# A Fourier mixing layer with an expert MLP: first load, spectrum layout and last tiles changed

## The chip, the cores and the metric

The kernel runs on one core of one Trainium2 chip. The time is the device time of one execution in microseconds. A profile of one execution gives the span from the first to the last instruction and what each engine did. The engines are TensorE (PE), VectorE (DVE), ScalarE (ACT), GpSimd (POOL) and SyncE (SP). SP, ACT and POOL can issue DMAs.

## The reference, cut to what matters

x has 8 batches of 2496 positions with 256 channels.

```python
X = np.fft.rfft(x, axis=1)
Yr = Xr @ w_r - Xi @ w_i + b_r          # complex 256 x 256 product per frequency
Yi = Xr @ w_i + Xi @ w_r + b_i
Y* = sign(Y*) * max(|Y*| - 0.01, 0)     # soft threshold of both parts
y = np.fft.irfft(Y, n=2496, axis=1)
e = argmax(mean(y, axis=1) @ w_gate)    # one expert of 8 for each batch
out = gate * (relu(y @ w1[e]) @ w2[e])  # 256 -> 1024 -> 256
```

## The kernel before

The transform of 2496 positions is split as 39 x 64. A batch goes through these steps; the names are those of the tiles, the lines those of the profile.

- x is loaded as `xin` (L265) from POOL's DMA queue, cast to fp16 on the way. Batch 0 is loaded in nine pieces, three groups of columns times three groups of 39 partitions; other batches in three.
- The DFT over 39 gives `pa`. In batches 0 and 1 ("direct", L424) it is evacuated into `XB` (L435). In batches 2 to 7 (L537) it goes to `A` (L547), is written to DRAM as `fwd` (L559, L564) and read back in another order as `XB` (L578), since the second transform needs other partitions.
- Direct batches multiply with the weights first (`pm` L460, evacuated as `Pt` L471) and then make the DFT over 64 (`pb` L488 and L490, with the tables `tf` and `tm`). The others make the DFT first (`px` L601, evacuated as `XT`), then three products (`pm` L639) that DVE joins with the bias (`tt` L653, `z` L662).
- DVE thresholds `z` into `Y` (L513 or L681).
- The inverse transform over 64 with the table `ti` gives `pv` (L382), evacuated as `V` (L390), two frequencies at a time. Each V is stored to the DRAM tile `scr` (L395). When all ten are stored, four DMAs read them back with the frequencies on 120 partitions (`V2`, L708 and L711; the profile cuts the number off and calls this tile V as well).
- The inverse over 39 with `wi` gives `pi` (L734), evacuated as `ysb` (L749, L755): y of the batch.
- The MLP goes over chunks of 512 positions, the last of 448. Eight pairs of matmuls per chunk give `ph` (L863), relu makes `hs` (L875 on ACT, L877 on DVE), and `po` (L896) multiplies with the second weights, scaled by the gate on evacuation into `ost` (L928 or L931) and stored from SP (L952).
- The last chunk leaves a tile of 64 rows. Its eight products (L907) go in two halves of four to PE columns 0 to 63 and 64 to 127, so that they can run beside each other; ACT evacuates the tile before (L928), DVE scales one half (L938) and adds the other (L941), and SP stores both (L957, L959).

The expert is found from the zero frequency as soon as that is there; POOL then reads its index and loads the weights `w1s` and `w2s` (L815, L820).

The order of all instructions is written out by a planner (`Schedule`). Each operation has an engine, a guessed duration, what it depends on, and a due time `vt`. The planner goes through simulated time, picks the engine (ACT or DVE) for evacuations, and emits the instructions in the order that it found. Times at which the first loads land are given to it as constants (`X0_AT`, `X1_AT`, `W_AT`, `T_AT`). What it emits on an engine runs in that order, each instruction waiting for its semaphores. PSUM has five banks for tag "a", two for "h" and one for "o". The load of x of batch b is held until `V2` of batch b-2 has been read: a POOL copy of one element of V2 into the new `xin` tile stands ahead of it.

Of the kernel before, what the change touches and what calls it, by code (L numbers as in the profile page):

```python
# [16 lines left out]
P = 128  # L17
B = 8
# [16 lines left out]
def _tables():  # L35
# [22 lines left out]
    wi = wi.reshape(120, 117)  # L58
# [9 lines left out]
    tf[:, :, 0, 1], tf[:, :, 1, 1] = -s * sg, c * sg  # L68
    def lay(m):
        return np.ascontiguousarray(  # L70
            m.reshape(NK1, P, P).transpose(1, 0, 2)).astype(np.float16)
# [11 lines left out]
    return wa.astype(np.float16), wi.astype(np.float16), lay(tf), lay(ti)  # L83
# [21 lines left out]
class Schedule:  # L105
# [17 lines left out]
    def op(self, eng, occ, emit, vt, deps=(), lat=None, allocs=(), dma=0.0):  # L123
        o = Op((eng,), {eng: occ}, {eng: occ if lat is None else lat}, emit, vt,
               list(deps), list(allocs), dma)
        self.ops.append(o)
        return o
# [32 lines left out]
    def run(self):  # L160
        free = dict.fromkeys(("PE", "ACT", "DVE", "SP", "POOL"), 7.0)
        ring = {"SP": 7.0, "POOL": 24.0}
# [44 lines left out]
def kernel(  # L207
# [14 lines left out]
    wa_np, wi_np, tf_np, ti_np = _tables()  # L222
    d_wa = nc.inline_tensor(wa_np, name="d_wa")
    d_wi = nc.inline_tensor(wi_np, name="d_wi")
    d_tf = nc.inline_tensor(tf_np, name="d_tf")
    d_ti = nc.inline_tensor(ti_np, name="d_ti")
# [9 lines left out]
    XROW = 2 * D + 16  # L236
    BUFS = {"XT": 2, "hs": 2, "z": 3, "V": 6}
# [19 lines left out]
    def load_now(b, cuts, hold=None):  # L257

        xin = xpool.tile([117, NG // 2, XROW], FP16, name="xin")
        if hold is not None:  # L260
            nc.gpsimd.tensor_copy(out=xin[0:1, 0, 0:2], in_=hold)
        xv = x[b].rearrange("(a n) c -> a n c", n=N2)
        for c0, c1 in zip(cuts, cuts[1:]):
            for j in range(3):
                nc.gpsimd.dma_start(  # L265
                    out=xin[39 * j : 39 * j + 39, c0:c1, 0 : 2 * D],
                    in_=xv[:, 21 * j + 2 * c0 : 21 * j + 2 * c1, :].rearrange(
                        "a (g i) c -> a g (i c)", i=2))
        return xin

    wa = cpool.tile([117, 120], FP16, name="wa")
    nc.sync.dma_start(out=wa, in_=d_wa.ap())
    xin0 = load_now(0, (0, 4, 8, NG // 2))
# [3 lines left out]
    nc.gpsimd.dma_start(out=wm, in_=w_i.rearrange("(t p) c -> p t c", p=P))  # L277
    tf = cpool.tile([P, NK1, P], FP16, name="tf")
# [6 lines left out]
    for k0, k9 in ((0, 4), (4, 12), (12, 20)):  # L285
        nc.gpsimd.dma_start(out=tf[:, k0:k9], in_=d_tf.ap()[:, k0:k9])
        nc.vector.tensor_scalar_mul(out=tm[:, k0:k9, 0:64],
                                    in0=tf[:, k0:k9, 64:P], scalar1=-1.0)
        nc.vector.tensor_copy(out=tm[:, k0:k9, 64:P], in_=tf[:, k0:k9, 0:64])
        if k0 == 0:  # L290
            for i, bv in enumerate((b_r, b_i)):
                nc.gpsimd.dma_start(
                    out=bias[:, i],
                    in_=bass.AP(tensor=bv.tensor, offset=bv.offset,
                                ap=[[0, P], [1, D]]))
        nc.gpsimd.dma_start(out=ti[:, k0:k9], in_=d_ti.ap()[:, k0:k9])
    bias2 = cpool.tile([P, D], FP32, name="bias2")
    nc.vector.tensor_copy(out=bias2[0:64], in_=bias[0:64, 0])
    nc.vector.tensor_copy(out=bias2[64:P], in_=bias[64:P, 1])
# [3 lines left out]
    nc.vector.tensor_copy(out=w4[:, :, 2], in_=wr)  # L303
    nc.scalar.copy(out=w4[:, :, 3], in_=wm)  # L304
    nc.vector.tensor_sub(out=w4[:, :, 0], in0=wm, in1=wr)
    nc.vector.scalar_tensor_tensor(out=w4[:, :, 1], in0=wr, scalar=-1.0, in1=wm,
                                   op0=ALU.mult, op1=ALU.subtract)
# [6 lines left out]
    xin1 = load_now(1, (0, NG // 2))  # L314
# [3 lines left out]
    nc.vector.tensor_copy(out=wg16, in_=wg)  # L318


    X0_AT, X1_AT = (9.5, 12.0, 14.0), 26.0
    W_AT, T_AT = 16.5, (18.0, 20.0, 21.0)
# [15 lines left out]
    w_in = [S.fixed(W_AT)]  # L338
# [6 lines left out]
    xdone = {0: [S.fixed(t) for t in X0_AT], 1: [S.fixed(X1_AT)]}  # L345
# [7 lines left out]
    def add_load(b):  # L353
        def emit(_):

            hold = V2_t[b - 2][0:1, 20, 0:2]
# [5 lines left out]
        o.after = xdone[b - 1][0] if b > 2 else None  # L362
# [9 lines left out]
    def add_inverse_b(b, k0, cell, oy, vt):  # L372
# [14 lines left out]
        def ev(eng):  # L387
            if b not in scr_t:
                scr_t[b] = dpool.tile([P, NK1, D], FP16, name="scr")
# [4 lines left out]
        def st(_):  # L394
            nc.sync.dma_start(out=scr_t[b][:, k0 : k0 + 2, :], in_=hc["V"])  # L395
# [5 lines left out]
    def add_attn_direct(b):  # L401
# [5 lines left out]
        for gb in range(6):  # L407
            gs = range(4 * gb, min(4 * gb + 4, NG))
            nq = 12 if gb < 5 else 4
            for ch in range(2):  # L410
# [3 lines left out]
                def mm(_, gs=gs, ch=ch, cell=cell):  # L414
# [6 lines left out]
                    for i, g in enumerate(gs):  # L421
# [7 lines left out]
                         vt(0.02 * gb), deps=[xd[min(gb // 2, len(xd) - 1)]],  # L429
# [14 lines left out]
        for kp in range(NK1 // 2):  # L444
# [61 lines left out]
            oz = S.op("DVE", 0.61, z_, v, deps=[m], lat=0.74)  # L506
# [15 lines left out]
    def add_attn(b):  # L522
# [61 lines left out]
        for q in range(NQ):  # L584
# [42 lines left out]
            for t in (2, 1, 0):  # L627
# [3 lines left out]
                def mm(_, t=t, cell=cell):  # L631
# [5 lines left out]
                    for a in range(2):  # L637
                        for ch in range(2):
# [7 lines left out]
                                deps=([so] if t == 2 else [m_ops[2]]) + w_in,  # L646
# [51 lines left out]
    def add_inverse_a(b, v_ops, vt):  # L698
        V2k = S.tok("V2", 2)
        r_ops = []  # L700
        for h in range(4):
            def rd(_, h=h):
# [3 lines left out]
                sv = scr[0:126].rearrange("(g q) k c -> (q k) g c", q=6)  # L706
                if h < 3:
                    nc.sync.dma_start(out=V2[:, 7 * h : 7 * h + 7, :],  # L708
                                      in_=sv[:, 7 * h : 7 * h + 7, :])
                else:  # L710
                    nc.sync.dma_start(  # L711
                        out=V2[:, 21, :],
                        in_=scr[122:128].rearrange("q k c -> (q k) c"))
            r_ops.append(S.op("SP", 0.4, rd, vt(0.88), deps=v_ops,
                              dma=1.9 if h < 3 else 0.4,
                              allocs=[V2k] if h == 0 else []))
# [3 lines left out]
        for gb in range(6):  # L720
            gs = range(4 * gb, min(4 * gb + 4, NG))
            for ch in range(2):
# [3 lines left out]
                def mm(_, gs=gs, ch=ch, cell=cell):  # L726
# [4 lines left out]
                    for i, g in enumerate(gs):  # L731
# [5 lines left out]
                need = r_ops[: min((4 * gb + 3) // 7, 2) + 1] if gb < 5 else r_ops  # L737
                va = (vt(0.9 + 0.02 * gb) if b < 1
                      else (b + LATE + 0.01 * gb) * PERIOD)
                m = S.mm(cols, mm, va,  # L740
                         deps=need, after=m if y_ops else None,
# [20 lines left out]
    def add_gating(b, cell, oy, v):  # L762
# [25 lines left out]
        m = S.mm([60, 60], ml, v, deps=[e], allocs=[k2_])  # L788
# [56 lines left out]
    def add_moe(b, y_ops, yk, gate):  # L845
        w, gb_op, wk = gate
        v0 = b * PERIOD
        for c, (ns, nl) in enumerate(NCH):
# [32 lines left out]
            for sp in range(2):  # L881
                half = nl < 512 and sp == 1
                tago = "o" if b < B - 1 else "h"
                ok = S.tok(tago, BANKS[tago])
                oc = {}
                for q in range(3 if half else 4):
                    v = v0 + PERIOD * (c * 8 + 6 + 4 * sp + q) / 44

                    def mm(_, sp=sp, q=q, cell=cell, oc=oc, tag=tago):
                        if q == 0:  # L890
                            oc["p"] = bank("po", tag).rearrange(
                                "p (i c) -> p i c", i=2)
                        i = q // 2
                        s0 = (2 * sp + i) * P
# [6 lines left out]

                    def mm_half(_, cell=cell, oc=oc):


                        for ft in (0, 4, 1, 5, 2, 6, 3, 7):
                            s = 64 * (ft // 4)
                            nc.tensor.matmul(  # L907
                                oc["p"][s : s + 64, 1, :],
                                cell["hs"][:, ft, 384:448],
                                w2s_t[b][:, ft, :],  # L910
                                start=(ft % 4 == 0), stop=(ft % 4 == 3))
                    m = S.mm([256] * (6 if q == 2 and half else 4),
                             mm_half if q == 2 and half else mm, v,
                             deps=h_ops[: 8 if q == 2 and half
                                        else 4 + 4 * (q % 2)],
                             after=m2 if q else None,
                             allocs=[ok] if q == 0 else [])
                    m1, m2 = (m2 if q else None), m
# [3 lines left out]
                def ev(eng, oc=oc, half=half):  # L922
                    oc["o"] = ost = opool.tile([P, 2, D], FP32, name="ost")
                    o, i = ost, oc["p"]
                    if half:
                        o, i = ost[:, 0], oc["p"][:, 0]
                    if eng == "ACT":
                        nc.scalar.activation(out=o, in_=i, func=AFT.Copy,  # L928
                                             scale=gbc_t[b])
                    else:  # L930
                        nc.vector.tensor_scalar_mul(out=o, in0=i,  # L931
                                                    scalar1=gbc_t[b])
                e = S.evac(280 if half else 560, ev, v,
                           deps=[m1 if half else m2, gb_op])
                ok.rel.append(e)
                if half:
                    def ev1(_, oc=oc):
                        nc.vector.tensor_scalar_mul(  # L938
                            out=oc["o"][0:64, 1], in0=oc["p"][64:P, 1],
                            scalar1=gbc_t[b][64:P])  # L940
                        nc.vector.scalar_tensor_tensor(  # L941
                            out=oc["o"][0:64, 1], in0=oc["p"][0:64, 1],
                            scalar=gbc_t[b][0:64], in1=oc["o"][0:64, 1],
                            op0=ALU.mult, op1=ALU.add)
                    e = S.op("DVE", 0.8, ev1, v, deps=[m2, e], lat=0.9)
                    ok.rel.append(e)

                def st(_, ns=ns, nl=nl, sp=sp, oc=oc, half=half):
                    ost = oc["o"]
                    r0 = ns + 256 * sp  # L950
                    if not half:
# [4 lines left out]
                    else:  # L956
# [3 lines left out]
                                          in_=ost[0:64, 1, :])  # L960
                S.op("SP", 0.6 if half else 0.3, st, v, deps=[e], dma=0.75)
# [35 lines left out]
```

## Time and profile before

| what | value |
|---|---|
| times of 3 runs | 441.29, 441.54, 445.46 us; median 441.54 |
| profiled execution | 441.54 us, span 439.9 |
| PE busy | 419.4 us (95%) |
| DVE, ACT busy | 294.9, 324.8 us |
| first matmul | 8.04 us after the start of the span |
| end of the last matmul | 434.94 us |
| DMA | 99,785 packets, 79.18 MB, mean 180 GB/s |
| reading V2 back | 24 DMAs of 420 KB, median 7.2 us to landing |
| a load of x, batches 1 to 7 | 429 KB each, median 9.4 us to landing |

A group's row gives line, engine, operation, out<-in and count; then busy time, mean ns of one, idle time of the engine before it and who ended that. A timeline row begins with start and duration in us. A row of stretches gives start:end, length, the busy time of PE, its weight loads, DVE, ACT and POOL (number of instructions in brackets), the granted share of the TensorE clock, the mean share of the 16 DMA engines and GB/s. A row of the chain of waits gives start, duration and what the kernel's end hung on at that time.

### The profile page before, as it was taken

The page shows a single profiled execution, that of the slowest core. Times are in us where ns is not written, and L with a number is a line of the kernel's source. Part 1 is how long each engine was busy: PE and PEld are TensorE (multiplying, and loading weights), DVE is VectorE, ACT ScalarE, POOL GpSimd, SP SyncE. Part 2 cuts the span into 40 slices and gives each one's busy share as a digit, 9 for nine tenths or more (in the row PEclk, how much of TensorE's full clock was granted, in tenths as well). Part 3 has the DMA queues.
Part 4 walks back from the last instruction along what each step waited for, and adds up shares of the span by engine and source line. Part 5 has one row for each costly group of instructions (what it writes and reads, how often), then busy time and mean ns, then how long its engine had stood idle before and what let it go on. Part 6 is the DMA issues. An engine that isn't in the chain of part 4 may idle for free.

```text
span 439.9 us, 9039 instructions
## 1 busy us (share of the span) xinstructions
PE 419.4 (95%) x3378; PEld 296.5 (67%) x3378; DVE 294.9 (67%) x627; ACT 324.8 (74%) x633; POOL 41.9 (10%) x66
## 2 busy tenths in 40 slices
PE   1998999999999999999999999999999999999995
PEld 1555566676777866777677866778667777676663
DVE  0697847498867887687976788687976877323010
ACT  2598977687867867778867787677777788677773
POOL 7510300020001100021000200021000010000000
PEclk9999999999999999999999999999999999999998
DMA  8997996999879986899879997699978583471222
GB/s 115 266 163 172 205 192 170 241 193 219 203 242 201 193 171 182 238 190 223 183 239 209 171 200 200 211 199 206 186 206 217 145 164 101 127 154 67 72 73 91
DMA packets 99785, 79.18 MB, mean 180 GB/s; under 512 B 8165, under 2 KB 93341, under 8 KB 99741
## 3 DMA queue, kind: packets, MB, share of 16 engines
q1 hardware_dynamic: 75421, 57.56, 48.6%
q0 software_dynamic: 24320, 21.04, 30.8%
q8 instruction: 26, 0.43, 0.4%
q14 instruction: 18, 0.15, 0.1%
HBM read 58.71 MB, written 38.80 MB: 222 GB/s over the span
## 4 chain that ended last, share of the span: by engine, by line
PE 66%; DVE 13%; DMA 12%; issue 4%; ACT 2%; POOL 1%; SPq 1%; DVEq 0%; POOLq 0%; ACTq 0%
PE po L896 25%; PE ph L863 23%; DMA xin<-in_x_dram 7%; PE pm L639 6%; DMA V<-scr 5%; PE pi L734 3%; PE pv L382 3%; PE px L601 2%; DVE Y L681 2%; DVE z L662 2%; PE pm L460 1%; POOL xin L265 1%; PE pa L537 1%; DVE tt L653 1%; DVE z L502 1%
## 5 line engine op out<-in xcount | busy, mean ns | idle before, releaser
L875 ACT ACTIVATE hs<-ph 128x512 f16<-128x512 f32 (+1 forms) x298 | 170.9, 592 | 70.7 <-PE ph L863 67.6
L863 PE MATMUL ph<-ysb,w1s 128*128 128x512 f16 (+1 forms) x640 | 179.0, 374 | 0.5 <-ACT ysb L755 0.5
L896 PE MATMUL po<-w2s,hs 128*128 128x256 f16 x1216 | 172.9, 272 | 0.0
L896 PEld LDWEIGHTS <-hs 128*128 128x128 f16 x1216 | 117.1, 98 | 50.9 <-issue 2.0
L863 PEld LDWEIGHTS <-w1s 128*128 128x128 f16 x640 | 61.3, 98 | 22.6 <-issue 1.0
L928 ACT ACTIVATE ost<-po,gbc 128x512 f32<-128x512 f32 x78 | 52.0, 667 | 12.1 <-PE po L896 7.5
L681 DVE TENSOR_TENSOR Y<-z,cl 64x512 f16<-64x512 f16 x120 | 50.4, 420 | 2.7
L639 PE MATMUL pm<-w,XT 128*128 128x256 f16 x360 | 49.5, 273 | 0.7
L653 DVE TENSOR_TENSOR tt<-pm,bias 128x512 f16<-128x512 f32 x60 | 38.5, 682 | 15.3 <-PE pm L639 15.2
L639 PEld LDWEIGHTS <-XT 128*128 128x128 f16 x360 | 34.1, 98 | 12.8 <-issue 2.9
L662 DVE TENSOR_TENSOR z<-pm,tt 128x512 f16<-128x512 f32 x60 | 38.4, 678 | 2.5 <-PE pm L639 2.4
L877 DVE TENSOR_SCALAR hs<-ph 128x512 f16<-128x512 f32 (+1 forms) x22 | 15.1, 685 | 30.6 <-PE ph L863 30.4
L547 ACT CAST A<-pa 120x512 f16<-120x512 f32 x46 | 26.8, 608 | 7.7 <-PE pa L537 7.7
L749 DVE CAST ysb<-pi 128x468 f16<-128x468 f32 (+1 forms) x37 | 20.9, 585 | 16.7 <-PE pi L734 16.5
L390 ACT CAST V<-pv 128x512 f16<-128x512 f32 x50 | 29.7, 598 | 1.9 <-PE pv L382 1.4
L749 ACT CAST ysb<-pi 128x468 f16<-128x468 f32 (+1 forms) x59 | 27.3, 535 | 2.3 <-PE pi L734 2.2
L382 PE MATMUL pv<-Y,ti 128*128 128x256 f16 x160 | 27.0, 272 | 1.8 <-DVE Y L513 1.3
L609 DVE CAST XT<-px 128x512 f16<-128x512 f32 x27 | 18.2, 688 | 15.7 <-PE px L601 15.7
L460 PE MATMUL pm<-w,XB 128*128 128x512 f16 x80 | 23.5, 410 | 1.9 <-ACT w L304 1.0
L390 DVE CAST V<-pv 128x512 f16<-128x512 f32 x30 | 20.5, 683 | 5.5 <-PE pv L382 5.5
L734 PEld LDWEIGHTS <-V 120*128 120x128 f16 x352 | 21.0, 98 | 4.1 <-issue 0.7
L734 PE MATMUL pi<-wi,V 120*128 120x117 f16 x352 | 23.1, 214 | 0.4 <-ACT ysb L749 0.2
(69 smaller groups left out, 347.3 us busy)
## 6 DMA issues: line engine op xcount, KB each, us to landing
out_dram<-ost SPq DMA_DIRECT2D x72, 256.0 KB, 2.7
scr<-V SPq DMA_DIRECT2D x80, 128.0 KB, 2.9
V<-scr SPq DMA_DIRECT2D x24, 420.0 KB, 7.2
xin<-in_x_dram POOLq DMA_DIRECT2D x21, 429.0 KB, 9.4
XB<-fwd SPq DMA_DIRECT2D x30, 256.0 KB, 3.7
fwd<-A SPq DMA_DIRECT2D x18, 360.0 KB, 3.5
w1s<-in_moe_w_dram POOLq DMA_DIRECT2D x8, 512.0 KB, 9.8
w2s<-in_moe_w_dram POOLq DMA_DIRECT2D x8, 512.0 KB, 8.4
```

The source lines that it names most:

```text
L382: nc.tensor.matmul(pv[:, D * i : D * i + D], ti[:, k0 + i, :], cell["Y"](i))
L390: COPY[eng](out=hc["V"].rearrange("p i c -> p (i c)"), in_=hc["p"])
L639: nc.tensor.matmul(pm[:, D * a : D * a + D], cell["X"][:, ch, a, t].rearrange("p i k -> p (i k)"), w4[:, ch, t, :], start=(ch == 0), stop= ...
L653: nc.vector.tensor_add(out=cell["tt"][:, r], in0=cell["T", 2].rearrange("p (a c) -> p a c", a=2), in1=bias[:, r].unsqueeze(1).to_broadcast ...
L662: nc.vector.tensor_add(out=cell["z"][:, r], in0=cell["T", 1 - r].rearrange("p (a c) -> p a c", a=2), in1=cell["tt"][:, r])
L681: nc.vector.tensor_sub(out=Y[64 * r : 64 * r + 64, :, i], in0=cell["z"][s, r], in1=cell["cl"][s, r])
L734: nc.tensor.matmul(pi[:, 117 * i : 117 * i + M], V2[:, g, ch * P : ch * P + P], w)
L749: COPY[eng](out=yv[:, :, 12 * gb : 12 * gb + 3 * nf].rearrange("p a (g j) -> p a g j", j=3), in_=pi[:, 0 : 117 * nf].rearrange("p (g a j) ...
L863: nc.tensor.matmul(ph[:, 0:nl], w1s_t[b][:, ch, fc * P : fc * P + P], ysb_t[b][:, ch, ns : ns + nl], start=(ch == 0), stop=(ch == 1))
L875: nc.scalar.activation(out=o, in_=i, func=AFT.Relu)
L896: nc.tensor.matmul(oc["p"][:, i, :], cell["hs"][:, ft, s0 : s0 + P], w2s_t[b][:, ft, :], start=(ft == 0), stop=(ft == E - 1))
L928: nc.scalar.activation(out=o, in_=i, func=AFT.Copy, scale=gbc_t[b])
```

## The change

Four things change together.

1. *Start.* The first four column groups of x of batch 0 are loaded as fp32 into a free `hs` buffer, by four DMAs from SP's queue and two from ACT's (39 rows of 4 KB each), and cast by ACT and DVE. The rest stays on POOL's queue. Nine matmuls on a zeroed tile stand first in PE's stream. The table `tm`, made by DVE before, is loaded (three more DMAs). Weight casts, the bias halves and the gate's cast become planned operations; two weight products go from DVE to POOL.
2. *Spectrum.* `scr` is stored as [frequency, position, channel] instead of [position, frequency, channel], with the position order of `ti` and `wi` changed so that a residue group of 21 positions is contiguous. It is read back in five parts by frequency (six in batch 0), planned behind the stores that each part needs, and one DMA for the last positions. All `pi` products wait for all parts.
3. *64-row tile.* The packed form goes. The tile takes the last 128 positions of the chunk, 64 of them for the second time, with ordinary products, one evacuation and a store of rows 64 to 127.
4. *Last tile of the last batch.* Its two halves get a bank each; DVE scales the first and SP stores it, ACT scales the second and stores it from its own queue.

The core of the diff:

```diff
+    xf = hpool.tile([117, 4, 2 * D], FP32, name="hs")
+    def x0_part(eng, j, c0, c1, dst):
+        eng.dma_start(
+            out=dst[39 * j : 39 * j + 39, c0:c1],
+            in_=xv[:, 21 * j + 2 * c0 : 21 * j + 2 * c1, :].rearrange(
+                "a (g i) c -> a g (i c)", i=2))
+    warm = cpool.tile([P, 512], FP16, name="warm")
+    nc.vector.memset(warm, 0.0)
+    x0_part(nc.sync, 0, 0, 2, xf)
+    x0_part(nc.scalar, 1, 0, 2, xf)
+    x0_part(nc.sync, 2, 0, 2, xf)
+    nc.scalar.dma_start(out=wa, in_=d_wa.ap())
+    x0_part(nc.sync, 0, 2, 4, xf)
+    x0_part(nc.scalar, 1, 2, 4, xf)
+    x0_part(nc.sync, 2, 2, 4, xf)
+    for c0, c1 in ((4, 8), (8, 11)):
+        for j in range(3):
+            x0_part(nc.gpsimd, j, c0, c1, xin0)
...
+    pw = psum.tile([P, 512], FP32, tag="o", name="po", bufs=BANKS["o"])
+    for _ in range(WARM):
+        nc.tensor.matmul(pw, warm[:, 0:P], warm)
...
-        nc.gpsimd.dma_start(out=tf[:, k0:k9], in_=d_tf.ap()[:, k0:k9])
-        nc.vector.tensor_scalar_mul(out=tm[:, k0:k9, 0:64],
-                                    in0=tf[:, k0:k9, 64:P], scalar1=-1.0)
-        nc.vector.tensor_copy(out=tm[:, k0:k9, 64:P], in_=tf[:, k0:k9, 0:64])
+        for t, d in ((tf, d_tf), (tm, d_tm)):
+            nc.gpsimd.dma_start(out=t[:, k0:k9], in_=d.ap()[:, k0:k9])
...
+    def w_products(_):
+        nc.gpsimd.tensor_sub(out=w4[:, :, 0], in0=wm, in1=wr)
+        nc.gpsimd.tensor_scalar_mul(out=wr, in0=wr, scalar1=-1.0)
+        nc.gpsimd.tensor_sub(out=w4[:, :, 1], in0=wr, in1=wm)
+    w_late = S.op("POOL", 4.0, w_products, 1.0, deps=list(w_in))
...
-                scr_t[b] = dpool.tile([P, NK1, D], FP16, name="scr")
+                scr_t[b] = dpool.tile([NK1, P, D], FP16, name="scr")
...
-            nc.sync.dma_start(out=scr_t[b][:, k0 : k0 + 2, :], in_=hc["V"])
+            nc.sync.dma_start(
+                out=scr_t[b][k0 : k0 + 2].rearrange("k p c -> p k c"),
+                in_=hc["V"])
...
-        for h in range(4):
...
-                sv = scr[0:126].rearrange("(g q) k c -> (q k) g c", q=6)
-                if h < 3:
-                    nc.sync.dma_start(out=V2[:, 7 * h : 7 * h + 7, :],
-                                      in_=sv[:, 7 * h : 7 * h + 7, :])
...
-            r_ops.append(S.op("SP", 0.4, rd, vt(0.88), deps=v_ops,
+        cuts = (0, 4, 8, 12, 16, 18, 20) if b == 0 else (0, 4, 8, 12, 16, 20)
+        for k0, k9 in zip(cuts, cuts[1:]):
...
+                nc.sync.dma_start(
+                    out=V2[6 * k0 : 6 * k9, 0:21, :],
+                    in_=scr[k0:k9, 0:126].rearrange("k (q g) c -> k q g c", q=6))
+                if k9 == NK1:
+                    nc.sync.dma_start(out=V2[:, 21, :],
+                                      in_=scr[:, 122:128])
+            r_ops.append(S.op("SP", 0.4 if k9 < NK1 else 0.8, rd,
+                              vt(0.1 + 0.04 * k9),
+                              deps=v_ops[k0 // 2 : k9 // 2],
+                              after=r_ops[-1] if r_ops else None,
...
-                need = r_ops[: min((4 * gb + 3) // 7, 2) + 1] if gb < 5 else r_ops
-                         deps=need, after=m if y_ops else None,
+                         deps=r_ops, after=m if y_ops else None,
...
-                        for ft in (0, 4, 1, 5, 2, 6, 3, 7):
-                            s = 64 * (ft // 4)
-                            nc.tensor.matmul(
-                                oc["p"][s : s + 64, 1, :],
-                                cell["hs"][:, ft, 384:448],
-                                w2s_t[b][:, ft, :],
-                                start=(ft % 4 == 0), stop=(ft % 4 == 3))
+                        s0 = min((2 * sp + i) * P, nl - P)
...
+                def ev_last(_, ns=ns, nl=nl, sp=sp, oc=oc):
+                    nc.scalar.activation(
+                        out=ost[64:P, 1], in_=oc["p", 1][64:P, 1],
+                        func=AFT.Copy, scale=gbc_t[b][64:P])
+                    nc.scalar.dma_start(out=out[b, r0 + P : ns + nl, :],
+                                        in_=ost[64:P, 1, :])
+                def ev_first(_, ns=ns, sp=sp, oc=oc):
+                    nc.vector.tensor_scalar_mul(
+                        out=ost[:, 0], in0=oc["p", 0][:, 0], scalar1=gbc_t[b])
+                    nc.sync.dma_start(out=out[b, r0 : r0 + P, :],
+                                      in_=ost[:, 0, :])
```

## The prediction

> **What bounds the kernel now.** I read the busy table first, then the stretches, then the timeline of both ends, then the chain of waits.
>
> ```profile
> PE 419.4 (95%) x3378; PEld 296.5 (67%) x3378; DVE 294.9 (67%) x627; ACT 324.8 (74%) x633; POOL 41.9 (10%) x66
> ```
> ```profile
> 0.00:8.00 8.00, 0.00 (x0) 0.00 (x0) 0.23 (x1) 1.28 (x1) 6.58 (x14) 1.00 0.74 90
> 8.00:15.00 7.00, 4.79 (x45) 4.30 (x46) 2.59 (x5) 4.59 (x10) 5.34 (x10) 1.00 1.12 271
> ...
> 155.00:206.00 51.00, 50.76 (x424) 36.84 (x423) 39.90 (x83) 38.78 (x76) 4.17 (x7) 1.00 0.89 199
> ...
> 435.00:440.00 5.00, 0.00 (x0) 0.00 (x0) 0.97 (x2) 0.47 (x1) 0.00 (x0) 0.71 0.28 93
> ```
> The second number of a row is PE's busy time. In a middle batch PE is busy 50.76 of 51 us: there only PE's own work counts. PE has nothing to do for 8.0 us at the start and 5.0 at the end. I also went from the start of each matmul to the start of the next: 407 us are work at 0.109 us per 256 columns and 19.7 us are lost between matmuls, 7.5 of them before 22 us, 7 from 22 to 75.
>
> ```profile
> 8.04 1.76 PE L424 MATMUL pa<-wa,xin 117*128 117x120 f16 x16 [8.04 <-DMA xin<-in_x_dram]
> 14.91 3.57 PE L460 MATMUL pm<-w,XB 128*128 128x512 f16 x8 [0.96 <-ACT w L304]
> 19.65 0.68 DVE L502 TENSOR_TENSOR z<-pb,bias 128x512 f16<-128x512 f32 x1
> 20.77 1.03 PE L460 MATMUL pm<-w,XB 128*128 128x512 f16 x4
> 434.31 0.63 PE L907 MATMUL po<-w2s,hs 128*64 128x256 f16 x8
> 435.03 0.47 ACT L928 ACTIVATE ost<-po,gbc 128x256 f32<-128x256 f32 x1 [0.31 <-PE po L907]
> 436.06 0.48 DVE L941 SCALAR_TENSOR_TENSOR ost<-po,gbc,ost 64x256 f32<-64x256 f32 x1
> 436.56 0.47 SPq L959 DMA_DIRECT2D out_dram<-ost x1
> ```
> At 14.9 us a 512-column matmul follows the last after 0.43 us, from 20.8 after 0.22. The granted clock reads 1.00 in both stretches, so it is the spacing that shows the slow array.
>
> ```profile
> 154.97 0.48 ACT ost L928
> 155.48 0.50 DVE ost L938
> 156.00 0.48 DVE ost L941
> 156.48 0.66 DVE tt L653 x2
> ```
> ```profile
> 40.47 9.18 DMA V<-scr
> 50.41 1.60 POOL xin L265 x2
> 52.01 14.22 DMA xin<-in_x_dram
> ```
> In the chain of waits the 64-row tile's three evacuations stand in a row ahead of the next batch's DVE work, and the spectrum's read-back releases the load of x two batches on.
>
> **The change, part by part.** Its own time for the profiled execution is 441.54, the median of the three; the span is 439.9, so 1.6 lie around it.
>
> *Start.* The first four column groups of x come as six fp32 pieces on the SP and ACT queues. SP's first issue stood at 0.88, and later SP issues took 0.4 to 0.5 each. Small SP loads landed 3.5 to 3.9 us after issue there, XB 3.7, out 2.7; I take 3, so the first half lands at 4.3, the second at 5.3. Casts: 0.42 on DVE, 0.63 on ACT (rows L303, L304), ACT after its table load (1.28). PE reaches x at 5.2, not 8.0. The rest of x stays on POOL: now 9 loads land from 5.43 to 12.65, the last six are left; the pieces share the DMA engines, so I expect 9 us for units 4 to 7 and 11.2 for the end of x. Weights follow behind (13.1 and 13.9 now): 11.7 and 12.5. The first L460 product waits for the ACT cast of them: 13.2 instead of 14.9.
> The nine dummies are 9 x 0.43 = 3.9 us of slow spacing, from 1.3 to 5.2, where PE is idle anyway: cost nothing; if x were there at 3.5 they would cost 1.7. Dummies and pa products then fill about 5.5 us, and before, the array turned fast after 5.8 us without a gap (14.9 to 20.7), so I take it as fast at 13.2. Those 5.8 us then cost half.
> Queues: ACT has bias2's two copies (0.28 each on DVE) and wg's ahead of the Pt evacuations; the bias lands 4.5 and 3.9 us after issue at about 9.7 and 10.3, so 14.2, and Pt on ACT stands until 14.6. First z then at about 16.0, against 19.65: **-3.6 us**. Ends: -1.5 (array still slow, pieces late) and -5.0. z's come every 1.7 us up to 35 us with ACT and DVE over 90% busy, so the gain passes through but does not grow. POOL has three tm loads more ahead of xin of batch 1 (0.7 + 1.4 + 1.4 us of packets on 16 engines); its cover, 26.65 (landed) to 32.72 (first use), is used up to about 0.5 us. POOL's three weight products, now ahead of the expert's index and loads: 0.68 us each on DVE, on POOL perhaps five times that, so 2 to 10 us; w1s landed at 33.2 and is used at 53.6, which hides either.
>
> The Trainium skill (TensorE: Matmul & The Clock Gate, The HAM clock gate) says that a free-running window of about 3.4 us of activity speeds the array and an idle window of that length slows it. By it the dummies and the pa products after them would be enough even if the first window is cut; the trace needed 5.8 us without a gap. By the rule the -3.6 stands; with an array that is still slow at 13.2 it is -1.5 and the sum 442.6.
>
> *64-row tile.* The packed form (L907, 8 matmuls) takes 0.65 us of PE, entry and exit gaps of 0.09 included; eight full 256-column matmuls take 8 x 0.109 = 0.87. +0.22 x 8 = **+1.8**. Gone are 0.48 + 0.50 + 0.48 us in a row on ACT and DVE, for one 0.69 on ACT. What stands behind them on DVE is tt, then pv's input: in the batch from 155 PE loses 0.30 at 161.7 and 0.27 at 167.7. Ends 0 and -0.57 for each of six batches; the planner has reshuffled the evacuations, so I take a third, **-1.2**.
>
> *Spectrum.* The stores (L395) keep their bytes but write 512-byte rows: 2560 packets a batch for 1280. The trace's packet records give 46 ns for 1024 bytes and 40 for 512: 6.4 us an engine for 3.7, hidden as the landing (2.9) is waited for only by the reads. The reads (L708, L711) had 2640 rows of 512 bytes; now 120 of 10,752 and 120 of 512, in five or six parts that follow their stores. Nearest row: 2048 bytes in 84 ns, so 0.44 us a row. How many engines share a part decides:
>
> ```profile
> DMA packets 3141, 1.94 MB, mean 177 GB/s; under 512 B 92, under 2 KB 2988, under 8 KB 3140
> ```
> From 39 to 50 us, 92 four-byte packets end four 120-row reads and two 128-row stores: 4 x 15 + 2 x 16, and over the run the 4144 of that queue fit the same count, the largest divisor up to 16 of the outermost rows. A part has 24 rows in SBUF, but 4 x 6 in DRAM: 12 engines (2 rows, 0.9 us) or 4 (6 rows, 2.6 us). All transfers so far split on whole outermost steps of both sides, so I take 4.
> Batch 0 leaves four parts and the last row group behind the last store (SP order): 4 x 2.6 = 10.6 us on the busiest engines, from about 36 (39.5 now, less 3.6), so all have landed at 47. PE reaches the first pi after 29.7 us of its work instead of 27.1, at 46.5; all pi now wait for all parts: +0.5. x of batch 2 is released then and takes 14.5 us, to 62.5; PE wants it at 61.5: +0.9. Batch 1 puts three parts (8 us) ahead of the XB reads on SP; XB had 2.7 us of room: +1.0. Sum **+2.4**; with 12 engines 0.
> Middle batches: the last part lands about 4 us sooner than the four reads (9.6 us from issue to release now), but the first pa stands 4.7 us of PE work earlier relative to pi, and x landed 1.0 to 1.5 us ahead of it. About 0.1 a batch, **+0.6**; ends 0 and +9.
>
> The Trainium skill speaks against this part too (DMA: Bandwidth & Descriptors, Why a DMA increments its semaphore by 16): the engine count must divide the outermost size of both sides, and a hardware queue uses the lowest-numbered engines. The count of 92 agrees where both sides have the same size; no transfer of this trace has unequal sides. By the rule there are 4 engines, always the same ones, and the sum is 440.5; by the SBUF side alone it would be 438.1 or, with nothing lost in the middle batches, 437.5.
>
> *End.* After PE's last matmul (434.94) ACT, DVE, DVE, SP issue at 436.56: 1.62 us. Now the first half is scaled under the last 8 matmuls, and ACT scales 64 rows (0.47) and issues the store itself: 0.6. **-1.0**; if the ACT queue issues slower than SP, -0.5.
>
> Sum: -3.6 + 1.8 - 1.2 + 2.4 + 0.6 - 1.0 = -1.0: **440.5 us**.
>
> **Rivals.** (a) *Slower: the engines that carry the parts run full.* Share 0.89 of a 51 us batch is 45 us per engine. Four engines lose 7 us of old reads and get 30 x 0.44 = 13.2 and 2.7 from the stores: 54 in 51. From the point at which an engine holds no more than its share 1.0, XB and x come late in each batch, 1.5 us or more, six times: 450. Against it: shares of 1.24 at 4 to 7 us show that packets overlap. (b) *Parts spread and hidden, DVE relief in full:* without +2.4 and +0.6, 437.5; with -3.4 for -1.2, 435.3. For it: 10 KB rows, and parts that land with the work. Against: the count of engines. (c) *The start does less than it says:* array still slow at 13, or bias late: -1.5 for -3.6, 442.6. For it: 12.7 us from the first load to a fast array before.
>
> **How the numbers follow.** Forecast (438.5 to 443.5) 0.50, (a) 0.22, (b) 0.16, (c) 0.12. A measurement of this kernel tells about 1% (4.4 us) from no change. Faster than 437.1 is most of (b): 0.15. Slower than 446 is (a) and a little more: 0.23. The range runs from (b)'s better half to (a): 436 to 449.
>
> **What would show it.** pa's first matmul near 5.2 us, L460's first near 13.2 and at 0.22 us spacing, z near 16; 44 pi in one run near 47; last store issued 0.6 us after PE. Wrong if: middle batches are longer than 51.2 us with PE waiting for XB or xin (a); V2's parts land within 4 us of issue (b); z later than 18 (c).

## The result and the profile after

The changed kernel takes 487.56 us (median of 4 runs, 484.83 to 492.74) beside 442.20 for the kernel before on the same chip: ratio 1.099, 95% interval 1.090 to 1.108. I had forecast 440.5 with a range up to 449. The profiled execution is the longest of the four (492.74 us, span 491.1), so stalls read from it come to a little more than the ratio, which leaves it out as disturbed.

The table of busy times and four of the stretches, columns as before:

```profile
PE 439.2 (89%) x3387; PEld 306.8 (62%) x3387; DVE 290.4 (59%) x609; ACT 329.0 (67%) x633; POOL 45.4 (9%) x69
```
```profile
8.00:15.00 7.00, 4.47 (x40) 3.40 (x38) 2.89 (x6) 4.37 (x10) 4.14 (x8) 1.00 0.98 238
...
175.00:180.00 5.00, 5.00 (x20) 3.04 (x21) 1.18 (x3) 0.60 (x1) 0.00 (x0) 0.50 0.34 87
180.00:229.00 49.00, 48.16 (x396) 34.92 (x395) 37.20 (x78) 36.89 (x71) 4.27 (x6) 0.99 0.77 184
229.00:234.00 5.00, 0.65 (x9) 0.45 (x7) 0.93 (x3) 1.32 (x5) 0.00 (x0) 0.83 0.96 213
234.00:239.00 5.00, 5.00 (x21) 2.95 (x20) 1.38 (x3) 0.60 (x1) 0.00 (x0) 0.50 0.22 55
```

PE's share fell from 95% to 89%, yet DVE, ACT and the DMA engines are less busy too. A middle batch now has a hole: PE stands from 229 to 234, then does 21 matmuls in 5 us at a granted clock of 0.50. The first `pa` of batches 4 to 7 start at 175.0, 233.8, 294.2 and 352.2 us, 58 to 60 us apart; before it was 50.7 (157.5, 208.2, 258.9, 309.6). From the start of each matmul to the start of the next, 77.1 us are lost (counted from the first dummy at 1.3 us), against 19.7 before.

The waits of PE (line, what it waited for, us in total, times, longest):

```profile
PE pa L600 <- DMA xin<-in_x_dram: 20.7, 5, 5.1
PE px L664 <- DMA XB<-fwd: 8.7, 6, 3.6
PE pi L799 <- DMA scr<-V: 6.5, 1, 6.5
```

Before, the first was 0.6 us in two, and the other two were not there. The timeline of one middle batch, with its SP and POOL issues and the PE rows that wait:

```profile
202.55 2.24 SPq L641 DMA_DIRECT2D XB<-fwd  x5
205.38 1.46 SPq L456 DMA_DIRECT2D scr<-V  x2
206.86 0.40 PE L664 MATMUL px<-tf,XB 128*128 128x128 f16 x4 [0.84 <-DMA XB<-fwd]
211.36 0.65 SPq L770 DMA_DIRECT2D V<-scr  x1
217.50 2.24 POOL L277 DMA_DIRECT2D xin<-in_x_dram  x3 [0.35 <-issue]
233.78 0.65 PE L600 MATMUL pa<-xin,wa 117*120 117x512 f16 x1 [4.35 <-DMA xin<-in_x_dram]
```

The same chain in three kernels, in us after the first matmul of the batch's last `pv` (at 229.5, 203.7 and 232.8); the third kernel is explained below:

| | before | after | merged_late |
|---|---|---|---|
| last store of V issued | 1.4 | 2.8 | 2.3 |
| last part (before: first read) issued | 3.3 | 7.7 | 5.3 |
| load of x issued | 13.4 | 13.8 | 9.6 |
| x landed | 28.2 | 29.8 | 23.7 |
| PE reaches the first `pa` | 29.4 | 25.7 | 29.6 |

I had expected the part-wise read to release x about 4 us sooner. It releases it no sooner (13.8 for 13.4) and x lands 1.6 later, while the new order brings PE to `pa` 3.7 us earlier. So PE stands, and the clock falls: at 0.50 a 512-column matmul follows after 0.43 us for 0.22. Behind the four longest stands for x (4.4 to 5.1 us) the granted clock stays at 0.50 for another 2.9 to 6.1 us of work. By the spacing I estimate that this costs some 1.5 to 3 us more each time.

The start and the end of the changed kernel in the timeline:

```profile
5.43 1.28 ACT L400 ACT_TABLE_LOAD   x1 [5.43 <-DMA hs<-in_x_dram]
6.73 0.62 ACT L400 CAST xin<-hs 117x512 f16<-117x512 f32 x1
7.40 0.98 PE L487 MATMUL pa<-wa,xin 117*128 117x120 f16 x8 [2.07 <-ACT xin L400]
15.37 3.57 PE L523 MATMUL pm<-w,XB 128*128 128x512 f16 x8 [0.96 <-ACT w L371]
19.91 0.69 DVE L565 TENSOR_TENSOR z<-pb,bias 128x512 f16<-128x512 f32 x1 [2.79 <-PE pb L553]
486.52 1.03 PE L962 MATMUL po<-w2s,hs 128*128 128x256 f16 x8 [0.39 <-ACT ost L979]
487.64 0.47 ACT L1003 ACTIVATE ost<-po,gbc 64x256 f32<-64x256 f32 x1 [1.17 <-PE po L962]
488.14 0.55 ACTq L1006 DMA_DIRECT2D out_dram<-ost  x1
```

ACT loads its table only when the first x has landed, and casts after that (the kernel before had loaded the table at 0.87). The first z comes at 19.9, not at 16.0 (19.65 before), and the mixing matmuls still follow at 0.43 us. The last store is issued 0.59 us after PE's last matmul, as forecast, but PE waits 0.39 us for a bank just before.

### The profile page after: what moved, and what is told of

It is laid out like the page before. It is cut to its first block, busy times and chain, and to the rows that moved or that the text cites. A ratio compares the mean times of both kernels' runs of the same rounds, so it can differ in the third digit from the quotient of the medians.

```text
span 491.1 us, 9073 instructions
## 1 busy us (share of the span) xinstructions
PE 439.2 (89%) x3387; PEld 306.8 (62%) x3387; DVE 290.4 (59%) x609; ACT 329.0 (67%) x633; POOL 45.4 (9%) x69
## 4 chain that ended last, share of the span: by engine, by line
PE 49%; DMA 35%; DVE 8%; issue 2%; ACT 2%; POOL 2%; SPq 1%; POOLq 0%; ACTq 0%; DVEq 0%
PE ph L927 17%; PE po L962 17%; DMA xin<-in_x_dram 16%; DMA V<-scr 8%; DMA scr<-V 6%; PE pm L702 5%; DMA XB<-fwd 3%; PE pa L600 3%; PE pv L443 2%; DVE z L565 2%; PE pi L799 2%; PE pm L523 1%; PE px L664 1%; DVE Y L576 1%; DMA fwd<-A 1%
## 5 line engine op out<-in xcount | busy, mean ns | idle before, releaser
L939 ACT ACTIVATE hs<-ph 128x512 f16<-128x512 f32 (+1 forms) x291 | 167.8, 591 | 107.5 <-PE ph L927 102.5
L962 PE MATMUL po<-w2s,hs 128*128 128x256 f16 x1280 | 186.1, 278 | 0.4 <-ACT ost L979 0.4
L927 PE MATMUL ph<-ysb,w1s 128*128 128x512 f16 (+1 forms) x640 | 183.5, 381 | 0.5 <-ACT ysb L819 0.5
L962 PEld LDWEIGHTS <-hs 128*128 128x128 f16 x1280 | 125.8, 100 | 55.5 <-issue 6.3
L702 PE MATMUL pm<-w,XT 128*128 128x256 f16 x360 | 51.7, 279 | 0.4 <-DVE XT L683 0.3
L941 DVE TENSOR_SCALAR hs<-ph 128x512 f16<-128x512 f32 (+1 forms) x29 | 19.9, 687 | 45.4 <-PE ph L927 40.8
L600 PE MATMUL pa<-xin,wa 117*120 117x512 f16 x66 | 23.1, 404 | 20.7 <-DMA xin<-in_x_dram 20.7
L813 DVE CAST ysb<-pi 128x468 f16<-128x468 f32 (+1 forms) x41 | 22.8, 577 | 25.7 <-PE pi L799 25.4
L451 ACT CAST V<-pv 128x512 f16<-128x512 f32 x54 | 31.7, 607 | 2.3 <-PE pv L443 1.9
L672 ACT CAST XT<-px 128x512 f16<-128x512 f32 x36 | 21.3, 598 | 9.8 <-PE px L664 9.5
L664 PE MATMUL px<-tf,XB 128*128 128x128 f16 x240 | 19.1, 220 | 8.7 <-DMA XB<-fwd 8.7
```

The source lines that it names most:

```text
L600: nc.tensor.matmul(pa[0:120, :], wa, xin_t[b][:, gp, 0 : 2 * D])
L702: nc.tensor.matmul(pm[:, D * a : D * a + D], cell["X"][:, ch, a, t].rearrange("p i k -> p (i k)"), w4[:, ch, t, :], start=(ch == 0), stop= ...
L813: COPY[eng](out=yv[:, :, 12 * gb : 12 * gb + 3 * nf].rearrange("p a (g j) -> p a g j", j=3), in_=pi[:, 0 : 117 * nf].rearrange("p (g a j) ...
L927: nc.tensor.matmul(ph[:, 0:nl], w1s_t[b][:, ch, fc * P : fc * P + P], ysb_t[b][:, ch, ns : ns + nl], start=(ch == 0), stop=(ch == 1))
L939: nc.scalar.activation(out=o, in_=i, func=AFT.Relu)
L962: nc.tensor.matmul(oc["p"][:, i, :], cell["hs"][:, ft, s0 : s0 + P], w2s_t[b][:, ft, :], start=(ft == 0), stop=(ft == E - 1))
```

## The experiments

Two theories after the first look. E: the few engines of each part hold up the spectrum and all that queues behind it. S: the start and the new order of work cost the time.

**rest: the spectrum part undone, start, full tile and end kept.** `scr`, `ti`, `wi` and the four reads are as before.

> The changed kernel with the spectrum part undone (old layout of scr, four reads of 120 rows behind the last store); the start, the full 64-row tile and the two-queue end stay. Theory E (the parts of the spectrum's read lie on 4 DMA engines; what queues behind them on those engines, V's stores and XB's reads, is late, so x is late and PE stands 4 to 5 us before pa in each batch and goes on with a slow array): PE waits for xin under 1 us in all, the period is back at 50.7 to 51.2, time 440 to 444, since the start brought the first z no earlier (19.91 against 19.65), the tile costs 1.8 and the end gives 1.0. Rival S (the new start or the new order of evacuations carries the loss): stays above 460.

442.41 us (4 runs), ratio 1.001 (0.999 to 1.004). S falls, and E stands so far: the whole loss is in the spectrum part, and the rest of the change gains nothing that can be measured. PE still waits 1.2 us for x, where I had written under 1.

**spec: the kernel before with the spectrum part alone.**

> The kernel before with the spectrum part alone. Theory E: the whole loss, 480 to 492, PE waiting about 20 us for xin in all. Rival S: 440 to 446.

494.14 us, ratio 1.119 (1.115 to 1.123). That confirms rest, though the time lies just above my range. Why it is 6.6 us above the full change stays open.

**merged: the parts on twelve engines.** The tile `scr` keeps only the 126 positions that the parts read, and the last six positions go to a tile of their own. Then the six rows of a frequency and those of the next follow at one step, and both sides of a part have 24 outermost rows:

```diff
-                scr_t[b] = dpool.tile([NK1, P, D], FP16, name="scr")
+                scr_t[b] = (dpool.tile([NK1, 126, D], FP16, name="scr"),
+                            dpool.tile([NK1, 6, D], FP16, name="scr6"))
...
-                    in_=scr[k0:k9, 0:126].rearrange("k (q g) c -> k q g c", q=6))
+                    in_=scr[k0:k9].rearrange("k (q g) c -> (k q) g c", q=6))
```

> The changed kernel, but scr holds 126 positions a frequency and the last six positions go to a tile of their own, so that the 24 rows of a part have one step in DRAM: rows of 10,752 bytes, parts, 512-byte stores and the planner's figures stay, ten small stores a batch are added. Theory E: the parts run on 12 engines (2 rows, 0.8 us), PE's wait for xin falls from 20.7 to under 2 us, time 438 to 446. Rival L (512-byte stores, or the order in which pa now stands earlier than x can come, make the loss, whatever the engines): above 465 still.

447.48 us (4 runs), ratio 1.013 (1.010 to 1.017): 40 of the 45 us are gone with the same 10,752-byte rows, parts and planner's figures. SP's queue shows the engine counts: a transfer ends in one 4-byte packet for each engine. The kernel before has 4144 of them. The change has 3927, which is 4 engines for a four-frequency part, 2 for a two-frequency one, 10 for the read of the last positions; with twelve for each part it would be 332 more. merged has 4619: 8 more for 39 parts, 10 more for the two short ones, 5 more for each of eight reads of the last positions, 6 for each of 80 small stores, 2 fewer for each of 80 long ones (126 rows, 14 engines): 312 + 20 + 40 + 480 - 160 = 692, exactly the difference. It is still above my range (446 at most, waits for x under 2 us). What is left is this row:

```profile
PE pa L604 <- DMA xin<-in_x_dram: 6.8, 5, 2.4
```

**two: ten parts of two frequencies each, on two engines.**

```diff
-        cuts = (0, 4, 8, 12, 16, 18, 20) if b == 0 else (0, 4, 8, 12, 16, 20)
+        cuts = tuple(range(0, 21, 2))
```

> The changed kernel with ten parts of two frequencies each in place of five of four. Theory E: each part lies on 2 engines, which then carry 60 rows x 0.41 = 24.5 us a batch instead of 12.3, beside the some 40 us of other packets: the two engines are full, 510 to 560. Rival L: the parts are finer and come earlier, so the time is that of the changed kernel or below, 475 to 490.

555.67 us, ratio 1.258 (1.254 to 1.262). The same 960 rows of 10,752 bytes, 60 a batch on an engine for 30, cost 114 us; PE waits 57.0 us for XB. Two, four and twelve engines: 556, 488, 447.

**poolread: the parts issued on POOL's queue, not SP's.**

```diff
-                nc.sync.dma_start(
+                nc.gpsimd.dma_start(
                     out=V2[6 * k0 : 6 * k9, 0:21, :],
...
-            r_ops.append(S.op("SP", 0.4 if k9 < NK1 else 0.8, rd,
+            r_ops.append(S.op("POOL", 0.4 if k9 < NK1 else 0.8, rd,
```

> The changed kernel with the parts of the read-back issued on POOL's queue, not SP's, and with nothing else changed; POOL has 32 more issues. It asks whether the loss is the order of one queue (spectrum stores and XB reads that stand behind parts in SP's queue) or the load of the few engines, whatever the queue. Theory Q, order of one queue: the XB waits of PE (18.3 us in the changed kernel) go to under 3 us, the wait of the last part for its spectrum store falls from 4.9 us to 2 to 3, pi waits fall from 6.5 in one, and the time is 450 to 465, because x, on POOL's own queue, still comes behind the parts. Theory E, the load of four engines: 30 rows of 0.41 us a batch still lie on them, stores and XB reads need those engines too, so the XB waits stay over 10 us and the time at 475 to 490. A third way: the software queue spreads the parts over other engines than SP's does; then the 10,752-byte packets are split up or lie on more engines, which the count of 4-byte records on the queue would show, and the time is below 450.

480.04 us, ratio 1.087 (1.084 to 1.091). The waits of PE:

```profile
PE pa L600 <- DMA xin<-in_x_dram: 28.3, 5, 8.4
...
PE px L664 <- DMA XB<-fwd: 0.6, 2, 0.4
```

So the XB waits (8.7 us in the change; the 18.3 that my expectation gives is a mistake) came from the parts on SP's queue: with the parts gone from it they vanish. By the ratios the move was worth 5 us in all, and the waits for x grew from 20.7 to 28.3. Theory Q's second marker failed: the last part is issued 8.2 us after the last store (193.46 to 201.62), not 2 to 3, and the time lies in theory E's range. POOL's own queue had a part issued at 190.20 that landed at 197.44. POOL has 49 more issues, not 32. How many engines POOL's queue gives a part, and which, I could not read from its packets, so the run does not separate the order of SP's queue from a change of engines.

**plan: the planner's figure for a part set to 0.65 us a frequency.** No transfer changes.

```diff
-                              dma=0.3 * (k9 - k0) + (0.4 if k9 == NK1 else 0),
+                              dma=0.65 * (k9 - k0) + (0.4 if k9 == NK1 else 0),
```

> The changed kernel with one figure of the planner set right: a part of the read-back is planned at 0.65 us a frequency and not at 0.3 (2.6 us a four-frequency part, which is what its 6 rows of 0.41 us an engine take); the program does the same transfers. Theory E, the few engines: the transfers are as slow, only the order of the engines' work fits them better; waits of PE for x fall by some 10 us at best, the XB waits stay over 10, and the time is 470 to 488. Rival P, the plan's wrong figure is the cause, since the order puts the next batch's first matmuls and the read of XB where data can't be yet: the time falls under 455 and pa waits under 5 us in all.

462.99 and 470.16 us, which are too far apart for a ratio. PE's wait for x is 6.8 us in three and for XB 0.7. Both theories missed: between 17 and 25 of the 45 us go away with the same four engines, once a part is not planned to be quicker than it is.

**merged_late: merged, with the planner's figure for a load of x at 12 us.**

```diff
-                 dma=7.0)
+                 dma=12.0)
```

> The twelve-engine version (merged) with the planner's figure of a load of x at 12 us, not 7; the transfers are the same. It asks what the last 5 us of that version are. Theory P: the plan puts pa of the next batch some 2 us ahead of the landing of x, five times, and each stand costs its own length; planned later, PE does other work first: waits for x under 3 us (6.8 in merged), time 441.5 to 445. Rival T: the added small stores and the engines' load hold back all else, and the time stays at 446 to 449, with the wait moved to another buffer.

443.69 us (10 runs), ratio 1.005 (1.003 to 1.006). P holds: PE has no stand for x in the middle batches, and 3.8 of merged's last 5 us are gone. In the table above x lands 5.9 us before PE reaches `pa`: the quicker read-back exists with twelve engines, and the time doesn't use it, since PE was full there already.

**plan_late: four engines, both figures corrected.**

> The changed kernel with both figures of the planner set to what the traces show: 0.65 us a frequency for a part, 12 us for a load of x. The transfers are the same, four engines for each part. It asks how much of the loss is left to the four engines themselves once no step is planned ahead of its data. Theory P+E, about half and half: waits of PE for x under 3 us (6.8 with the first figure alone), time 452 to 462. Rival P alone (a plan with right figures hides the four engines): 443 to 448. Rival E alone: no better than with the first figure, 464 to 470.

469.16 us (3 runs), ratio 1.062 (1.060 to 1.065). No further gain, and the time is that of rival E: waits for x are gone from the top of the list, but others take their place, `pv` for Y, `pi` for V, `pl` for the pooled sum. The first `pa` of batches 4 to 7 are now 53.2 to 53.8 us apart, still not the 50.7 of before. From here to merged_late there are 25 us. Both plans have 12 us for a load of x. For a part merged_late keeps 0.3 us a frequency, which suits its own transfers: two rows of 0.61 us for four frequencies. So 25 us is what four engines for twelve cost when each plan fits its transfers.

**fulltile: the kernel before with the full tile and the two-queue end alone.**

> The kernel before with the end of the change alone: the full 64-row tile in every batch, the last two tiles on two queues. My terms: +1.8 on PE, -1.2 from DVE, -1.0 at the end: 441.0 to 441.5 beside 441.7. Rival: in 51 us of a batch only PE counts and DVE's relief is worth nothing, and the end's gain is eaten by PE's wait for the second bank (0.4 to 0.55): 443 to 444.

441.58 us (12 runs), ratio 1.002 (1.0002 to 1.0036). By the ratio that is +0.1 to +1.6 us, nearer to the rival than to my -0.4, though the medians of the two kernels are alike (441.58 and 441.56). The run has all three terms together and does not tell which of them is off.

**rest_packed: the start alone**, with the packed tile and the old end.

> The kernel before with the start of the change alone: x in six pieces on two queues, nine dummy matmuls, weights cast later and products on POOL; the packed 64-row tile and the old end. My term was -3.6. Rival, from the trace of rest: z comes at 19.7 as before, since x as a whole and the weights land when they did and the clock is at half again by 15 us: 441 to 442.5, a gain under 0.7. What the full tile is worth comes out of the difference of rest and this.

442.81 us (12 runs), ratio 1.004 (1.002 to 1.006): a loss where I had written a gain of 3.6, and slower than the rival too. One reason why the dummies don't help shows in the stretches of rest, which has the same start:

```profile
7.50:8.10 0.60, 0.53 (x8) 0.43 (x8) 0.00 (x0) 0.12 (x2) 0.00 (x0) 1.00 1.11 270
8.10:10.40 2.30, 0.06 (x2) 0.00 (x0) 0.44 (x2) 0.91 (x2) 0.73 (x2) 0.75 1.10 202
10.40:14.30 3.90, 3.78 (x36) 3.40 (x36) 1.94 (x4) 2.62 (x6) 3.13 (x6) 0.50 0.99 275
```

The dummies end at 5.3 us, the first eight x products run fast at 7.6 (0.53 us), and PE stands for the second half of x until 10.4. The mean of 0.75 over 8.1 to 10.4 puts the fall to 0.50 at about 9.25, within that stand. In the profiles of rest_packed and of the change itself it is otherwise: there the same eight products take 0.98 us (at 7.70 and at 7.40), so nine dummies had not made the array fast at all. The same start can go either way.

**keepwarm: the kernel before, with dummies where PE stands cold.** 15 before x, then some between the groups of the first transform:

```diff
+                    if b == 0:
+                        for _ in range(2 if gb < 4 else 4 * ch * (gb == 5)):
+                            nc.tensor.matmul(pw, warm[:, 0:P], warm)
```

> The kernel before with dummy matmuls put where the array stands cold: 15 before x, two after each of the first eight groups of the first transform and four after the last; nothing else of the change. Theory C, the clock: the dummies of the change end at 5.3 us and their warmth is gone by 10.4; kept up to 14.9, the mixing matmuls run at 0.22 and not 0.43 us until 20.8, so z comes 1.5 to 2.5 us earlier and the time is 439 to 440.5. Rival D: z waits for weights and the work behind it for other transfers, DVE and ACT; the time stays at 441 to 442 though the matmuls are fast. If the dummies delay the first transform, pm comes later than 14.9 and the time grows by as much.

440.47 us (12 runs), ratio 0.998 (0.997 to 0.9997). C holds in kind: the mixing matmuls follow at 0.216 us. But z comes at 18.9, only 0.7 sooner, not 1.5 to 2.5. The mixing matmuls begin at 15.87 for 14.91, because the dummies hold up the last groups and the casts queue behind those.

**keepwarm2: fewer of them**, counts by group `(2, 2, 1, 1, 0, 5 * ch)[gb]`.

> As keepwarm, with fewer dummies behind x: two after each of the first four groups of the first transform, one after each of the next four, five after the last. In keepwarm the first mixing matmul came at 15.87 and not 14.91, because its dummies held up the last groups and with them the casts of the weights (ACT's at 15.2, 14.2 before). Theory C: with that delay gone the first mixing matmul comes at 14.9 to 15.2 at 0.22 spacing, z at 18.0 to 18.3 (18.9 in keepwarm, 19.65 before), the time 438.8 to 440.2. Rival D: from there on z waits for the tables or DVE is full (4.7 of 5 us from 15 to 20 in keepwarm), and the time is that of keepwarm, 440.5, or the clock falls back to half with fewer dummies, and it is 441.5.

440.05 us (12 runs), ratio 0.997 (0.995 to 0.999). Its timeline:

```profile
14.64 1.89 PE L468 MATMUL pm<-w,XB 128*128 128x512 f16 x8
17.70 0.68 DVE L510 TENSOR_TENSOR z<-pb,bias 128x512 f16<-128x512 f32 x1
```

Eight matmuls take 1.89 us and not 3.57, and z comes 1.95 us sooner. This version beats both kernels, by 0.3% of the time before.

## Why the prediction was wrong, step by step

*What bounds the kernel.* Right, and I drew too little from it. If only PE's own work counts in a middle batch, a read-back that is quicker can gain nothing there, and one that is late costs its whole length.

*Middle batches, +0.6 with ends 0 and +9: the step that failed.* "The last part lands about 4 us sooner" is the term that went wrong: it took the part to be issued as early as the first read was, and put the wait ahead of it at nothing. From its issue to the release of x the last part is indeed 4.0 us quicker (6.1 for 10.1, by the table). But it is issued 4.4 us later (7.7 for 3.3): the last store comes 1.4 later, and the part then waits 4.9 us after that store's issue (206.48 to 211.36; 1.9 before). So x is issued 0.4 us later than before and not 4 sooner. Why the stores land so late is not settled. They stand behind earlier parts in SP's queue, and each part holds its engines for 6 rows of 0.41 us; but with the parts on POOL's queue the wait was longer still (8.2). "The first pa stands 4.7 us of PE work earlier" was nearly right (3.7). Together they give a stand of over 4 us in each of the last four batches, and it recurs, as the planner is as wrong in each. From the first `pa` of batch 2 to that of batch 7 the change takes 279.2 us for 243.2, so +36.0. Even my upper end of 9 us was a quarter of that. The order that the planner wrote was in my hands, but I took its promise for the transfer time, 0.3 us a frequency, beside my own 0.65 and didn't ask what the difference does to the order. The runs price the two errors: with the planner's figures left, 4 for 12 engines costs 40 us; with them corrected, 25. The figure of the part alone is worth 17 to 25 of the 45 at four engines.

*Batches 0 to 2, +2.4.* Four engines was the right count, and the row time too (0.44 estimated, 0.41 measured). But I had all parts landed at 47; the last are issued at 46.4 and 47.1 and PE stands 6.45 us at the first `pi`, priced at 0.5. The first `pa` of batch 2 starts 6.7 us later than before, where the start and these batches together were to bring it 1.2 earlier.

The Trainium skill (DMA: Bandwidth & Descriptors, Why a DMA increments its semaphore by 16) let me count engines before any transfer with unequal sides had been seen; the packet counts of the change and of merged agree with it to the last packet. Its other statement, that a hardware queue uses the lowest-numbered engines, is not shown by any record here, since they don't name the engine.

*A term that was missing: the clock.* I priced the cold array at the start only. Each stand of 4 us and more for x is followed by 2.9 to 6.1 us of work at 0.50.

The Trainium skill (TensorE: Matmul & The Clock Gate, Part 1: The HAM clock gate) has an idle window of about 3.4 us for this, which fits the middle stands. At the start of rest no stand was that long: the clock fell at about 9.25 us, in a stand of 2.3 us behind one of 2.2 with only 0.6 us of work between. There the measurement decides, and a stretch that was mostly idle was enough.

*Start, -3.6.* Measured +0.8 to +2.7. The first half of x was ready for PE at 7.4, not 5.2. It lands at 5.4 for 4.3, and ACT's table load (1.28), which the forecast had ahead of the landing, stands behind it; why the landing is late was not tested. x as a whole and the weights come no earlier than they did. The array was cold at 15.4: "dummies and pa products then fill about 5.5 us" overlooked the two stands between them, and in the profile of the change the products from 7.4 on are slow already. POOL's three weight products took 1.26 to 1.61 us each, about twice DVE's 0.68 and not five times. Rival (c) had the mechanism at half the size.

*Tile and end, +1.8 - 1.2 - 1.0.* -0.4 expected, +0.1 to +1.6 measured for all three. The store is issued 0.59 us after PE as forecast; the wait for the bank gives 0.39 of it back. Which of the terms is off was not separated.

*Rival (a)* had the right sign, place and mechanism (XB and x late in each batch), with 1.5 us a batch where some 8 came. Whether its four engines ran full can't be read: the mean share of all 16 in the batch from 180 us is 0.77, and the records don't name the engine. Its sum of 54 us a batch for them is near the 53.2 to 53.8 of plan_late, where the plan fits the parts, which speaks for it. What it left out for the changed kernel are the late issue, the planner and the clock.

## What to carry to other kernels

Size a DMA by the engines that it runs on, and then look at what stands behind it in its queue and on these engines; long rows on four engines cost 45 us here (28 with the plan put right), on twelve 2 to 6. When an order is planned ahead, a wrong figure of the plan can be a stall that recurs, so compare the planner's numbers with the trace before trusting a new step. Dummy matmuls helped here when they went on up to the work that they were to speed, with no long stand between (the longest in keepwarm was 1.6 us), and when they were few enough not to delay what feeds it.

## What the runs showed of the hardware that I had not expected

- Transfers of one queue can delay others on it that have nothing to do with them: with parts on SP's queue PE waited 8.7 us for XB, without them 0.6. Whether the order of the queue does it or the engines that they share is not separated.
- In rest the granted clock fell to 0.50 within a stand of 2.3 us, with another of 2.2 shortly before. Behind stands of 4.4 to 5.1 us in the change it stayed there for 2.9 to 6.1 us of work.
- A row of 10,752 bytes took 0.41 us on its engine with four engines, and 0.61 with twelve (medians): spread wider, each row is slower and the whole far faster.
